# A Fourier transform ahead of a two-layer network: input folds written in place, and one more buffer for the units' differences

## The chip, the cores and the metric

The kernel runs on one core of one Trainium2 chip. The metric is the device time of one execution in microseconds (us); lower is better. A core has five engines that run beside each other: TensorE (PE in the profile, its weight loads PEld), VectorE (DVE), ScalarE (ACT), GpSimd (POOL) and SyncE (SP), which here only starts transfers (DMAs). SBUF is the working memory that all of them reach, PSUM the one in which TensorE puts its sums.

## The reference

```
x: (8, 3008, 256) f32, w_in: (256, 2048), w_out: (2048, 256)
X = fft(fft(x, axis=1), axis=2).real                 # (8, 3008, 256)
h = X.reshape(24064, 256) @ w_in                     # (24064, 2048)
g = where(h >= 1, h, where(h <= -1, 0, (h + 1)**2 / 4))
out = g @ w_out                                      # (24064, 256)
```

## The kernel before, in words

**The transform.** The host only reorders x. Per batch b, x comes in eight tiles `x_b_q` of 128 x 2 x 512 floats (512 KB each, `load_x`, line 126, DMA on line 130, issued by SyncE). A *fold* (`fold_x`, line 133) adds the two halves of a tile into `y_b_q` (line 138), 96 x 512; for q = 0 a second instruction takes their difference over 64 columns (`yd`, line 142). Folds run on GpSimd, but for four of the first batch, which run on VectorE. Stage 1 (`stage1_sums`, line 323) reads y with 4 matmuls for a tile (line 330), and the sums are copied to a tile z (line 360). Stage 2 (line 391) multiplies z (line 403) and splits the result into a high and a low part, `pqh` and `pql` (lines 177 and 178). `nyquist` makes one row a batch, written to DRAM and read back into `nyb` tiles (lines 383 and 388).

**The network.** Work is cut into *units* (b, k, f): batch, chunk k of 3 (482, 512 and 512 columns), and one of 16 groups of 128 hidden features; 384 units in all. `gemm1` (line 434) makes two PSUM tiles `uv` with three matmuls each (line 443), then VectorE makes `us` (line 446) and the two halves of `h`, us - uv and us + uv (lines 449 and 450): the unit's differences. ScalarE makes the tile `a` with two activations (lines 455 and 456). `activate` (line 459) has VectorE write min/max of a and h over h (line 470), ScalarE make `gh` of it (line 471) and GpSimd make `gl` = h - gh in two instructions (line 475); these last two are the last readers of h. `gemm2` (line 484) runs four units later and adds twelve matmuls (line 507) into four PSUM banks `acc`. When a chunk closes (its last f), the banks are evicted by VectorE and ScalarE (lines 514 to 518, traced at a raised priority, line 512) into `o` tiles, and stored (line 525).

**The weights** come as 64-bit floats in raw words and are converted in the first part of the run (`convert_*`, lines 205 to 247) on VectorE, ScalarE and GpSimd; w_in is multiplied with the second transform's matrix there (`fold_half`, line 286). `take_delta` (line 303) copies one row of that result to SBUF and `move_delta` (line 279) spreads it with four small DMAs over a column of `delta` (line 282). The first 24 units (`NATIVE`) multiply in full precision with one matmul in place of three.

**Buffers.** A tile is asked for with a tag, and a tag has a fixed number of buffers (`bufs`); whoever wants the next one waits until the last reader of the buffer's old content is done. Before the change: `y` has 3 buffers of 512 columns, shared by the folded tiles and the three rows of `take_delta`; `h` has 3 of 1024 columns, shared by the units and those converted weights that have no other place in `WORK` (line 103); `xt`, which the x tiles use, has 4, and four raw weight tiles pass through it too (line 102); x tiles 4 to 7 of the first batch lie in the four `gl` buffers.

**The order of the work.** The start is written out by hand: `START`, `AHEAD`, `AMID` and `STEPS` (lines 67 to 99) name steps by letter and number (`y1` and `g3` are folds, `p3` stage 1 of tile 3, `l12` a weight load, `r1` a delta row's DMAs), and `pin` (line 590) fixes the order of issue on each engine up to unit 24. From there on the framework's scheduler sets the order on each engine and on SyncE's queue, from priorities in the order of tracing and from when it takes operands and buffers to be free. The transform of the next batch is cut into pieces (`fft_pieces`, line 415) that are strewn between the units; `stage1` (line 365) folds a tile one piece ahead of its matmuls, and a load of tile q + 4 is traced right after the piece of tile q (lines 634 and 635). Batch 1's folds of tiles 0 to 3 are tied behind VectorE's latest instruction by hand (line 146).

Of the kernel before, what the change touches and what calls it, by code (L numbers as in the profile page):

```python
# [9 lines left out]
F32 = mybir.dt.float32  # L10
# [12 lines left out]
P = 128  # L23
XC = 8
GPC = 4
CH = 512
# [74 lines left out]
RAW = {0: "gh", 1: "gh", 2: "woh", 3: "woh", 4: "woh", 5: "woh", 6: "wol", 7: "wol", 8: "wol", 9: "wol"}  # L101
RAW |= {10: "xt", 11: "xt", 12: "xt", 13: "xt", 14: "pqh", 15: "pql"}
WORK = {1: "a", 3: "a", 4: "gl", 5: "gl", 7: "a", 8: "gl", 9: "gl", 11: "a", 12: "gl", 13: "gl", 15: "a"}
BUFS = {"h": 3, "a": 3, "gl": 4}

EARLY_BANKS = 12
BANK = {"s2_0_3": "acc3", "delta_1": "acc2"}
# [8 lines left out]
def fft_ffn_kernel(ctx: ExitStack, tc: tile.TileContext, x, cst, w_in, w_out, out):  # L116
# [3 lines left out]
    sb = ctx.enter_context(tc.tile_pool(name="sb", bufs=1))  # L120
# [12 lines left out]
    def fold_x(b, q, engine=None):  # L133

        t = xt.pop((b, q))
        engine = engine or nc.gpsimd
        y = sb.tile([96, CH], F32, tag="y", name=f"y_{b}_{q}", bufs=3)
        first = engine.tensor_tensor(y, t[:96, 0], t[:96, 1], op=ALU.add)  # L138
        yt[b, q] = y
        if q == 0:  # L140
            y = sb.tile([96, NA], F32, tag="yd", name=f"yd_{b}", bufs=1)
            engine.tensor_tensor(y, t[:96, 0, :NA], t[:96, 1, :NA], op=ALU.subtract)
            yt[b, "d"] = y
        return first.ins

    def fold_x_behind_vector(q):
        last = [ins for ins in traced if ins.engine == mybir.EngineType.DVE][-1]
        sync = mybir.DependencyInfo(mybir.DependencyClass.Sync, mybir.DependencyReason.DATA)
        tc.add_manual_dep(fold_x(1, q), last.name, sync, reason="beside VectorE's next steps")
# [55 lines left out]
    def convert_mantissa(n):  # L205
        raw = raws.pop(n)
        tag = WORK.get(n, "h")
        t = sb.tile([P, 2, CH], U32, tag=tag, name=f"cv_{n}", bufs=BUFS[tag])
        high = raw[:, :, 1]
# [91 lines left out]
        nc.scalar.activation(wh[m][:, cols], folds[n], AF.Copy, scale=inner if m else 1.0)  # L301

    def take_delta(f4):
        row = sb.tile([1, CH], F32, tag="y", name=f"row_{f4}", bufs=3)
        nc.scalar.activation(row, folds.pop(2 * f4 + 1)[0:1], AF.Copy)
        deltas[f4] = row

    def fold_low(n):
        f4, m = divmod(n, 2)
        cols = slice(f4 * CH, (f4 + 1) * CH)  # L310
        high = wh[m][:, cols].bitcast(F32)
        pt = folds.pop(n)
        if m == 1:
            nc.vector.scalar_tensor_tensor(wl[m][:, cols], pt, inner, high, op0=ALU.mult, op1=ALU.subtract)
            if f4:
                folds[n] = pt
                take_delta(f4)
        else:
            nc.vector.tensor_tensor(wl[m][:, cols], pt, high, op=ALU.subtract)
# [45 lines left out]
    def stage1(b, q):  # L365
        for p in range(q, min(q + 2, XC)):
            if (b, p) in xt and (b, p) not in yt:
                fold_x_behind_vector(p) if b == 1 and p < 4 else fold_x(b, p)
        stage1_sums(b, q)
        stage1_copy(b, q)  # L370
# [60 lines left out]
    def signs(i):  # L431
        return (slice(0, 1), slice(1, 2)) if i == n_units - 1 else (slice(0, 2),)

    def gemm1(i):
        b, k, f = units[i]
        n = WIDTH[k]
        hi, lo = pq[b, k]
        cols = slice(f * P, (f + 1) * P)
        uv = []
        for m in range(2):  # L440
            t = ps.tile([P, CH], F32, tag="uv", name=f"uv_{i}_{m}", bufs=3)
            for j, (w, r) in enumerate(((wh, hi), (wl, hi), (wh, lo))):
                nc.tensor.matmul(t[:, :n], w[m][:, cols], r[:, m, :n], start=(j == 0), stop=(j == 2))  # L443
            uv.append(t[:, :n])
        us = sb.tile([P, CH], F32, tag="us", name=f"us_{i}", bufs=2)[:, :n]
        nc.vector.scalar_tensor_tensor(us, nyb[b, k][:, :n], delta[:, f : f + 1], uv[0], op0=ALU.mult, op1=ALU.add)  # L446
        run_steps(AHEAD.get(i, ""))
        h = sb.tile([P, 2, CH], F32, tag="h", name=f"h_{i}", bufs=3)[:, :, :n]
        nc.vector.tensor_tensor(h[:, 0], us, uv[1], op=ALU.subtract)  # L449
        nc.vector.tensor_tensor(h[:, 1], us, uv[1], op=ALU.add)  # L450
        a = sb.tile([P, 2, CH], F32, tag="a", name=f"a_{i}", bufs=3)[:, :, :n]

        run_steps(AMID.get(i, ""))
        for sg in signs(i):
            nc.scalar.activation(a[:, sg], h[:, sg], AF.Relu, bias=half, scale=0.5)  # L455
            nc.scalar.activation(a[:, sg], a[:, sg], AF.Square)  # L456
        fronts[i] = h, a
# [82 lines left out]
    def piece_sums(n):  # L540
# [10 lines left out]
        "m": lambda n: nc.sync.dma_start(cm, cst[:, _OFF[2] :]),  # L551
        "x": lambda n: load_x(0, n),
        "y": lambda n: fold_x(0, n, nc.vector),
        "L": lambda n: load_x(1, n),
        "Y": fold_x_behind_vector,
# [27 lines left out]
    def run_steps(names):  # L583
        for s in names.split():
            steps[s[0]](int(s[1:] or 0))
# [17 lines left out]
    for i in range(n_units + LAG):  # L603
        if i < n_units:
            b, r = divmod(i, per)
            r0 = NEXT if b == 0 else 0
            if r == r0:
                pending = fft_pieces(b + 1) if b + 1 < NB else []
                done, total = 0, sum(w for w, _ in pending)
                if pending and b:  # L610
                    for q in range(4):
                        load_x(b + 1, q)
            gemm1(i)
            if b == 0 and units[i][2] == NFT - 2:
                load_parts(units[i][1])
            if 1 < i <= PINNED:
                activate(i - 1)
            if i >= PINNED:
                activate(i)
        first, _, then = STEPS.get(i, "").rpartition("|")  # L620
# [4 lines left out]
        if i < n_units:  # L625
            run_steps(then)
            change = units[i][2] == (FIRST if b == 0 else 0) + LAG
            while pending and (change or units[i][2] != (FIRST if b == 0 else 0) + LAG - 1 and done < total * (r + 1 - r0) / (per - r0)):
                change = False
                w, f = pending.pop(0)  # L630
# [65 lines left out]
```

## Time and profile before

| what | value |
|---|---|
| runs | 1738.72, 1739.39, 1734.0 us; median 1738.72 |
| the profiled execution | 1734.84 us, its span 1733.1 us |
| granted TensorE clock | 1.000 |
| TensorE | 1723.0 us busy, 99% of the span, 7804 matmuls |
| weight loads | 1392.1 us, 80% |
| VectorE | 1418.8 us, 82% |
| ScalarE | 1333.9 us, 77% |
| GpSimd | 1168.0 us, 67% |
| DMA | 80.89 MB, mean 47 GB/s |

The span reaches from the first to the last instruction; the time of the execution has a little more around it. Busy time is the time in which an engine had an instruction under way. A wait is idle time of an engine, put down to the instruction that ended it (`DVE h L449 <- POOL gl L475` is VectorE idle ahead of line 449 until a gl subtraction on GpSimd was done). Matmuls are pipelined and their ends are modelled, so two that follow each other overlap in the rows.

### The profile page before, as it was taken

The page shows a single profiled execution, that of the slowest core. Times are in us where ns is not written, and L with a number is a line of the kernel's source. Part 1 is how long each engine was busy: PE and PEld are TensorE (multiplying, and loading weights), DVE is VectorE, ACT ScalarE, POOL GpSimd, SP SyncE. Part 2 cuts the span into 40 slices and gives each one's busy share as a digit, 9 for nine tenths or more (in the row PEclk, how much of TensorE's full clock was granted, in tenths as well). Part 3 has the DMA queues.
Part 4 walks back from the last instruction along what each step waited for, and adds up shares of the span by engine and source line. Part 5 has one row for each costly group of instructions (what it writes and reads, how often), then busy time and mean ns, then how long its engine had stood idle before and what let it go on. Part 6 is the DMA issues. An engine that isn't in the chain of part 4 may idle for free.

```text
span 1733.1 us, 21482 instructions
## 1 busy us (share of the span) xinstructions
PE 1723.0 (99%) x7804; PEld 1392.1 (80%) x7804; DVE 1418.8 (82%) x1759; ACT 1333.9 (77%) x1561; POOL 1168.0 (67%) x801
## 2 busy tenths in 40 slices
PE   9999999999999999999999999999999999999998
PEld 6556888888888888888888888888888888888877
DVE  8997788888788887788887888878887788888886
ACT  6877777877778777887777777778778777777776
POOL 1125768776778667786678766778667766676775
PEclk9999999999999999999999999999999999999999
DMA  8133112110011100111011100111001000000000
GB/s 318 48 109 133 59 45 74 48 38 31 12 62 59 32 25 13 62 59 32 25 37 49 60 19 25 49 37 60 19 25 37 1 35 32 1 25 15 10 25 25
DMA packets 33738, 80.89 MB, mean 47 GB/s; under 512 B 4704, under 2 KB 9952, under 8 KB 33632
## 3 DMA queue, kind: packets, MB, share of 16 engines
q1 hardware_dynamic: 33596, 79.52, 13.2%
q8 instruction: 61, 1.00, 0.2%
q14 instruction: 45, 0.37, 0.1%
q10 hardware_dynamic: 36, 0.01, 0.0%
HBM read 51.70 MB, written 27.81 MB: 46 GB/s over the span
## 4 chain that ended last, share of the span: by engine, by line
PE 67%; ACT 20%; DVE 10%; issue 2%; DMA 0%; ACTq 0%; SPq 0%
PE acc L507 41%; PE uv L443 20%; DVE h L470 9%; ACT a L456 7%; ACT gh L471 7%; ACT a L455 5%; PE s L403 2%; PE s L330 2%; PE wps L293 1%; ACT z L360 1%; DVE h L450 0%; DVE h L449 0%; DMA raw<-in_moe_w_in_dram 0%; ACTq L471 0%; DVE o L518 0%
## 5 line engine op out<-in xcount | busy, mean ns | idle before, releaser
L475 POOL TENSOR_TENSOR gl<-h,gh 128x512 fp32r<-128x512 f32 (+1 forms) x716 | 1043.4, 1479 | 427.9 <-ACT gh L471 368.2
L470 DVE SCALAR_TENSOR_TENSOR h<-a,h 128x1024 f32<-128x1024 f32 (+2 forms) x361 | 541.5, 1500 | 237.1 <-ACT a L456 234.8
L471 ACT ACTIVATE gh<-h 128x1024 fp32r<-128x1024 f32 (+2 forms) x361 | 376.9, 1044 | 340.8 <-DVE h L470 317.4
L507 PE MATMUL acc<-gh,woh 128*128 128x512 f32 (+1 forms) x1440 | 570.2, 396 | 2.3 <-DVE o L518 2.2
L507 PE MATMUL acc<-gl,woh 128*128 128x512 f32 (+1 forms) x1440 | 563.6, 391 | 0.0
L507 PE MATMUL acc<-gh,wol 128*128 128x512 f32 (+1 forms) x1440 | 560.7, 389 | 0.0
L455 ACT ACTIVATE a<-h,biases 128x1024 f32<-128x1024 f32 (+1 forms) x385 | 431.8, 1122 | 23.3 <-DVE h L450 22.0
L456 ACT ACTIVATE a<-a 128x1024 f32<-128x1024 f32 (+1 forms) x385 | 399.4, 1037 | 7.6
L507 PEld LDWEIGHTS acc<-gh,woh 128*128 128x128 f32 x1440 | 270.7, 188 | 60.6 <-DVE o L518 5.7
L507 PEld LDWEIGHTS acc<-gl,woh 128*128 128x128 f32 x1440 | 271.3, 188 | 56.5
L507 PEld LDWEIGHTS acc<-gh,wol 128*128 128x128 f32 x1440 | 270.7, 188 | 54.7
L443 PE MATMUL uv<-pqh,wh 128*128 128x512 f32 (+1 forms) x768 | 308.6, 402 | 1.0 <-DVE h L450 1.0
L449 DVE TENSOR_TENSOR h<-us,uv 128x512 f32<-128x512 f32 (+1 forms) x384 | 260.0, 677 | 51.9 <-POOL gl L475 5.3
L443 PE MATMUL uv<-pql,wh 128*128 128x512 f32 (+1 forms) x768 | 299.2, 390 | 0.0
L443 PE MATMUL uv<-pqh,wl 128*128 128x512 f32 (+1 forms) x768 | 298.8, 389 | 0.0
L446 DVE SCALAR_TENSOR_TENSOR us<-nyb,delta,uv 128x512 f32<-128x512 f32 (+1 forms) x384 | 278.8, 726 | 10.8 <-PE uv L443 10.4
L450 DVE TENSOR_TENSOR h<-us,uv 128x512 f32<-128x512 f32 (+1 forms) x384 | 256.4, 668 | 0.0
L443 PEld LDWEIGHTS uv<-pqh,wh 128*128 128x128 f32 x768 | 144.2, 188 | 38.0 <-issue 4.3
L443 PEld LDWEIGHTS uv<-pqh,wl 128*128 128x128 f32 x768 | 144.2, 188 | 34.7 <-issue 5.4
L443 PEld LDWEIGHTS uv<-pql,wh 128*128 128x128 f32 x768 | 144.1, 188 | 30.2 <-DVE pql L178 0.4
L138 POOL TENSOR_TENSOR y<-x 96x512 f32<-96x512 f32 x60 | 108.1, 1802 | 25.9 <-PE s L330 14.0
L360 ACT ACTIVATE z<-s 64x192 f32<-64x192 f32 x240 | 81.7, 340 | 7.3 <-PE s L330 3.8
(64 smaller groups left out, 679.7 us busy)
## 6 DMA issues: line engine op xcount, KB each, us to landing
x<-in_x_dram SPq DMA_DIRECT2D x64, 512.0 KB, 3.5
out_dram<-o SPq DMA_DIRECT2D x26, 512.0 KB, 2.8
out_dram<-o SPq DMA_DIRECT2D x14, 482.0 KB, 2.9
nyb<-nyr SPq DMA_DIRECT2D x24, 256.0 KB, 3.3
raw<-in_moe_w_in_dram SPq DMA_DIRECT2D x4, 512.0 KB, 7.1
raw<-in_moe_w_out_dram SPq DMA_DIRECT2D x4, 512.0 KB
part<-o SPq DMA_DIRECT2D x4, 512.0 KB
os<-part SPq DMA_DIRECT2D x4, 512.0 KB, 5.8
```

What stands on the lines that cost most here:

```text
L138: first = engine.tensor_tensor(y, t[:96, 0], t[:96, 1], op=ALU.add)
L360: ins = nc.scalar.activation(dst, src, AF.Copy)
L443: nc.tensor.matmul(t[:, :n], w[m][:, cols], r[:, m, :n], start=(j == 0), stop=(j == 2))
L446: nc.vector.scalar_tensor_tensor(us, nyb[b, k][:, :n], delta[:, f : f + 1], uv[0], op0=ALU.mult, op1=ALU.add)
L449: nc.vector.tensor_tensor(h[:, 0], us, uv[1], op=ALU.subtract)
L450: nc.vector.tensor_tensor(h[:, 1], us, uv[1], op=ALU.add)
L455: nc.scalar.activation(a[:, sg], h[:, sg], AF.Relu, bias=half, scale=0.5)
L456: nc.scalar.activation(a[:, sg], a[:, sg], AF.Square)
L470: nc.vector.scalar_tensor_tensor(h[:, sg], a[:, sg], 1.0, h[:, sg], op0=ALU.min, op1=ALU.max)
L471: nc.scalar.activation(gh[:, sg], h[:, sg], AF.Copy)
L475: engine.tensor_tensor(gl[:, sg], h[:, sg], gh[:, sg].bitcast(F32), op=ALU.subtract)
L507: nc.tensor.matmul(acc[:, :n], w, g[:, sg], start=(begin and j == 0), stop=(last and j == len(terms) - 1))
```

## The change

For q = 1 to 7 the fold's sum is no longer put into a `y` tile but written over the tile's own first half, `t[:96, 0]`, and stage 1 reads it there. So the x buffer is held until those matmuls are done. For q = 0 a `y` tile stays, since the second instruction still needs both halves; `y` goes from 3 buffers to 1, still shared with the three rows of `take_delta`. The two buffers given up (512 floats a partition each) are as large as one `h` buffer, and `h` goes from 3 to 4, for the units and for the converted weights.

```
-BUFS = {"h": 3, "a": 3, "gl": 4}
+BUFS = {"h": 4, "a": 3, "gl": 4}
...
         t = xt.pop((b, q))
         engine = engine or nc.gpsimd
-        y = sb.tile([96, CH], F32, tag="y", name=f"y_{b}_{q}", bufs=3)
+        y = sb.tile([96, CH], F32, tag="y", name=f"y_{b}_{q}", bufs=1) if q == 0 else t[:96, 0]
         first = engine.tensor_tensor(y, t[:96, 0], t[:96, 1], op=ALU.add)
...
-        row = sb.tile([1, CH], F32, tag="y", name=f"row_{f4}", bufs=3)
+        row = sb.tile([1, CH], F32, tag="y", name=f"row_{f4}", bufs=1)
...
-        h = sb.tile([P, 2, CH], F32, tag="h", name=f"h_{i}", bufs=3)[:, :, :n]
+        h = sb.tile([P, 2, CH], F32, tag="h", name=f"h_{i}", bufs=4)[:, :, :n]
```

## The prediction

> **What bounds the kernel now.** I read the stretches first (columns: PE, weight loads, DVE, ACT, POOL, each with its busy us and its instructions, then the granted clock).
>
> ```profile
> core 0: us, PE busy (x) PEld busy (x) DVE busy (x) ACT busy (x) POOL busy (x), PEclk, DMA share, GB/s
> 0.00:25.00 25.00, 22.77 (x115) 15.29 (x116) 17.91 (x45) 14.39 (x33) 5.79 (x9) 1.00 0.89 329
> 25.00:150.00 125.00, 125.00 (x421) 74.06 (x421) 117.31 (x181) 98.41 (x135) 21.94 (x18) 1.00 0.30 107
> 150.00:1700.00 1550.00, 1546.64 (x7149) 1280.09 (x7149) 1261.93 (x1508) 1201.35 (x1373) 1125.85 (x766) 1.00 0.11 38
> 1700.00:1733.10 33.10, 28.55 (x123) 22.69 (x121) 21.68 (x27) 19.75 (x23) 14.39 (x10) 1.00 0.09 33
> ```
>
> Three regimes stand there. Up to 25 us the kernel loads. From 25 to 150 us VectorE is the tightest (117.31 of 125 us, while TensorE issues 421 matmuls, 3.4 in a us). From 150 us on TensorE is busy for 1546.64 of 1550 us and issues 4.6 in a us, at clock 1.00 throughout; VectorE has 288 us to spare there. A matmul that is held at its start can still count as busy, so I looked next at the waits between 165 and 1733 us: every wait of TensorE itself that sums to over 0.8 us (total us, times, longest), and those of the tiles that the change touches.
>
> ```profile
> POOL gl L475 <- PE acc L507: 48.5, 21, 2.3
> PEld acc L507 <- DVE o L518: 5.7, 10, 1.1
> DVE h L449 <- POOL gl L475: 5.3, 8, 1.1
> PEld uv L443 <- DVE h L450: 2.6, 6, 1.3
> POOL y L138 <- PE s L330: 2.4, 1, 2.4
> PE acc L507 <- DVE o L518: 2.2, 7, 0.6
> PEld ny L376 <- ACT a L455: 1.5, 4, 0.4
> PEld s L330 <- ACT z L360: 1.2, 4, 0.3
> PE uv L443 <- DVE h L450: 1.0, 2, 0.9
> PEld uv L443 <- DVE us L446: 1.0, 4, 0.3
> PEld acc L507 <- ACT o L516: 0.9, 2, 0.5
> ```
>
> The rows of TensorE (PE and PEld) sum to 16.1 us in 1568 us. Only 4.6 us of it (2.6 + 1.0 + 1.0) is a wait for the PSUM banks that the units' differences read. The row that the fourth buffer is aimed at is VectorE's own: it waited 5.3 us, in 8 places, for GpSimd to let go of an h tile. Last I read the chain that ended last, which is TensorE without a break up to the final eviction.
>
> ```profile
> 1714.60 13.96 PE acc L507 x60
> ```
>
> That busy TensorE is near its limit is borne out by its weight loads, which stand in the groups:
>
> ```profile
> L507 PEld LDWEIGHTS acc<-gl,woh 128*128 128x128 f32 x1440 | 271.3, 188 | 56.5
> L507 PEld LDWEIGHTS acc<-gh,woh 128*128 128x128 f32 x1440 | 270.7, 188 | 60.6 <-DVE o L518 5.7 <-ACT o L516 0.9 <-ACT a L455 0.6
> ```
>
> The idle time ahead of a load is 39 ns on average (56.5 us by 1440) in a group that names no releaser, and 42 ns in the one that names 7.2 us. It is a pitch that every load has, not a wait that a buffer ends, so I count the named waits alone. The Trainium skill's page "Perfetto Trace Analysis", section "Identifying the Most-Contended Engine", says that matmul busy time misleads and that the busy share of LDWEIGHTS tells the headroom. By that rule TensorE, with loads busy for 80% of the span, is not at its limit, and a wait taken from another engine could shorten the kernel in full; the trace speaks against it with the 39 ns.
>
> **The fourth buffer of h.** An h tile is written on lines 449 and 450, read by ScalarE, written over on 470, and freed by the second gl subtraction on GpSimd (475). With four, the write of unit i waits for gl of unit i-4 instead of i-3, so the 5.3 us of VectorE should go. That is not yet time: VectorE must have made TensorE late. The longest such case shows how it came about.
>
> ```profile
> 1159.67 0.66 DVE L449 TENSOR_TENSOR h<-us,uv 128x482 f32<-128x482 f32 x1
> 1161.53 2.58 DVE L470 SCALAR_TENSOR_TENSOR h<-a,h 128x964 f32<-128x964 f32 x1 [1.20 <-ACT a L456]
> 1164.03 0.65 DVE L450 TENSOR_TENSOR h<-us,uv 128x482 f32<-128x482 f32 x1
> ```
>
> The older unit's L470 stands between the two halves of the newer unit's h, waits 1.20 us for ScalarE, runs long, and L450 frees its bank only after 1164.03, 3.7 us after L449 ended. There the order on VectorE, which the scheduler chooses outside the written-out start, made the wait, not a missing h buffer. A fourth buffer lets the scheduler place L449 and L450 earlier, and may undo some of these cases. The gain is therefore between 0 and 4.6 us; I take 1.5 us, about a third, since the one case that I can follow (1.3 of the 4.6) had its h tile in hand.
>
> The other side of the same step: if L449 and L450 go first, L470 comes later by up to one pair, and with it gh and gl.
>
> ```profile
> L450 DVE TENSOR_TENSOR h<-us,uv x384: 643/675/685, 26.8 to 1717.4; 128x512 f32<-128x512 f32 x128, 128x482 f32<-128x482 f32 x64
> L470 DVE SCALAR_TENSOR_TENSOR h<-a,h x361: 687/1476/2683, 146.3 to 1722.8; 128x1024 f32<-128x1024 f32 x124, 128x964 f32<-128x964 f32 x56, 128x512 f32<-128x512 f32 x1
> ```
>
> A pair is about 1.35 us (2 x 0.675, min/median/max in ns). What covers it is that gl is made early: the first wait row has GpSimd waiting 48.5 us, 21 times, for TensorE to give back a gl buffer, and no row has TensorE waiting for gh or gl. Cost 0; if that cover were gone, each such unit would cost TensorE up to 1.35 us.
>
> **The fold in place.** Lines 137 and 138 keep the same instruction, shape and count on the same engine; only the destination changes, for q = 1 to 7.
>
> ```profile
> L138 POOL TENSOR_TENSOR y<-x 96x512 f32<-96x512 f32 x60 | 108.1, 1802 | 25.9 <-PE s L330 14.0 <-DVE wol L262 6.7 <-DVE cv L216 2.5
> 12.81 5.09 POOL L138 TENSOR_TENSOR y<-x 96x512 f32<-96x512 f32 x4 [11.55 <-PE s L330]
> x<-in_x_dram SPq DMA_DIRECT2D x64, 512.0 KB, 3.5
> ```
>
> No row shows an in-place fold. L470 above writes over one of its inputs on another engine, at 1476 ns for twice the columns; it gives no reason for a price either way. Bounds: between a fold of the four at the start (1.27 us, 5.09 by 4) and the mean of all (1.80 us) lies 0.53 us, so 60 folds could move by 32 us of GpSimd up or down, an engine that has 424 us to spare between 150 and 1700 us (1550 less 1125.85). On the end: 0.
>
> What does move is who frees what. Now a fold waits for a y buffer, which the matmuls of three tiles earlier free. After the change it waits only for its load, and that load waits for the matmuls of four tiles earlier rather than for their fold. On a middle batch (SyncE, TensorE, GpSimd, TensorE):
>
> ```profile
> 346.20 13.80 SPq L130 DMA_DIRECT2D x<-in_x_dram  x2
> 482.18 1.03 PE L330 MATMUL s<-cs,y 96*128 96x96 f32 x8
> 495.23 2.23 POOL L138 TENSOR_TENSOR y<-x 96x512 f32<-96x512 f32 x1
> 532.97 1.03 PE L330 MATMUL s<-cs,y 96*128 96x96 f32 x8
> ```
>
> The sixth tile's load goes out at 346.2 us today. Changed, it waits for the second tile's matmuls, which end at 483.2 us, and lands 3.5 us later, at 486.7. Its fold runs at 495.2 today and TensorE reads it at 533.0. So a load 137 us later is still 8.5 us ahead of the fold and, less 2.2 us for a fold, 44 us ahead of its reader: cost 0, and 44 us is the cover. Behind the waiting load on SyncE's queue stand output stores, nyr and nyb. They are queued by the same scheduler that sees the new release time, so I expect the load to be queued later rather than to hold them; if it does hold them, a store has until the next chunk closes, about 67 us: 16 units of 4.18 us, the 6 matmuls of uv and 12 of acc that follow each other in the chain.
>
> ```profile
> 1709.03 1.39 PE uv L443 x6
> 1710.42 2.79 PE acc L507 x12
> ```
>
> **The single y buffer.** It holds each batch's first fold and the three rows of the delta column. Two rows are gone long before the next; the tight place is the last row, whose four small DMAs must land before batch 1's first fold may write.
>
> ```profile
> 116.19 2.41 SPq L282 DMA_DIRECT2D delta<-row  x4
> 120.91 1.27 POOL L138 TENSOR_TENSOR y<-x 96x512 f32<-96x512 f32 x1 [2.51 <-DVE cv L216]
> 133.34 1.03 PE L330 MATMUL s<-cs,y 96*128 96x96 f32 x8
> DMA to landing us min/median/max: 1.9/2.0/2.0
> ```
>
> The last of them is issued by 118.6 and lands by about 120.6; the fold starts at 120.91, held by VectorE anyway, and is read at 133.34. Cost 0, between a gain of nothing and 1 us that stays hidden.
>
> **The start.** The first folds on GpSimd run back to back (the row from 12.81 on), and the slots of the x tiles go on to weight loads:
>
> ```profile
> 16.59 3.77 PE L330 MATMUL s<-cs,y 96*128 96x96 f32 x32
> 24.74 1.59 SPq L200 DMA_DIRECT2D raw<-in_moe_w_in_dram  x2
> ```
>
> The matmuls that will free the slots end at 20.4 us; the weight loads that take them leave at 24.7. The order there is written out and stays. VectorE, which bounds 25 to 150 us, loses and gains no instruction, and has no h wait in that stretch. Cost 0, and no gain.
>
> **Sum.** Against its own time the profiled run (1734.84 us, span 1733.1) becomes 1734.84 - 1.5 + 0 + 0 + 0 = 1733.3 us. That run lies 3.9 us below the median of the runs shown (1738.72, of 1734.0 to 1739.39), so for the median I say 1737.2 us.
>
> **The rivals.** *Faster.* The schedule is made anew, and a freer VectorE also reaches the evictions at the chunk closings sooner. The waits on these (5.7 + 2.2 + 0.9) and on h (4.6) hold 13.4 us; half of it gone is 6.7 us, 1732.0 us. For it: all of these end on VectorE or ScalarE, where order is everything. Against: from 150 us on VectorE is busy for 81% of the time, and the evictions already have a raised priority (line 512).
>
> *Slower.* The same new order puts an L449 and L450 pair of the next unit ahead of an eviction. TensorE needs those banks at once at a closing, so a pair there costs 1.35 us in full.
>
> ```profile
> L518 DVE COPY o<-acc 128x512 f32<-128x512 f32 (+1 forms) x48 | 32.0, 672 | 2.4 <-PE acc L507 2.4
> ```
>
> 48 copies, two at a closing, make 24 closings, 3 of them in the start. It decides from 4 of the 21 on (5.4 us); at 8 it adds 10.8 us, 1749.5 us. For it: at these closings TensorE already waits in 17 places. Against: the priority, and the mean of such a wait, 0.46 us (7.9 by 17), less than a pair. The Trainium skill's "SBUF — State Buffer", section "Who interferes with whom", adds a way to it: a VectorE instruction with two SBUF inputs contends with GpSimd's reads. By that rule L470 (a and h) may meet more of gl and the folds. The trace agrees so far as L470 goes up to 2683 ns and L450, with one input in PSUM, never over 685.
>
> *VectorE's wait counts in full.* Its 5.3 us come straight off the end, as they would if TensorE were not the bound: 1733.4 us, just beyond what a measurement tells. For it: weight loads leave TensorE's load path idle for some 40 ns each; against: the chain's end, and that only 4.6 us of TensorE's waits lie on what h frees. It is the rule of the Trainium skill's "Perfetto Trace Analysis" above that would have it so.
>
> *Nothing happens.* The h tiles wait on gl in 8 units only, and if the scheduler issues VectorE in the order of today, the fourth buffer stands empty: 1738.7 us.
>
> **How the numbers follow.** Forecast 0.54, nothing 0.10, faster 0.18, VectorE's wait in full 0.04, slower 0.14. A measurement of this kernel tells some 0.3%, or 5.2 us, from no change; the forecast and the last rival lie within it, so 0.22 faster, 0.64 same, 0.14 slower. The range goes from 1730 us (the faster rival's 1732.0 and a little of its other half) to 1743 us (three closings at 1.35 us above the highest run, 1739.39).
>
> **What would show it.** Right: the row of h waiting for gl is gone, TensorE's busy time from 150 to 1700 us stays within 2 us, its waits sum to 12 to 17 us, folds of a batch's last tiles come after loads that leave behind the matmuls of four tiles earlier, and the single y buffer makes no wait over 1 us. Wrong: a row in which TensorE waits for gl or for y, closings with waits over 1 us, output stores standing behind x loads so long that an eviction waits for its o tile, or a stretch from 25 to 150 us that is longer or shorter by over 2 us.

## The result, and the profile after

The change makes the kernel slower: the median goes from 1734.7 us (6 runs, 1732.1 to 1739.39) to 1757.92 us (6 runs, 1755.02 to 1765.07), a ratio of 1.0139 with a 95% interval of 1.0123 to 1.0155. The forecast was 1737.2 us in a range of 1730 to 1743; the time lies outside it. The profiled execution took 1756.21 us, its span is 1754.4 us at a granted clock of 1.000, so the comparison below is with the span of 1733.1 us. Three of the six runs after (1759.61 to 1765.07 us) had a mean granted clock of 0.997, the other three (1755.02 to 1756.23 us) one of 1.000.

The stretches of after come first, cut at the same times (columns as before: PE, weight loads, DVE, ACT, POOL).

```profile
0.00:25.00 25.00, 23.11 (x115) 15.41 (x116) 17.99 (x45) 14.32 (x33) 5.79 (x9) 1.00 0.91 327
25.00:150.00 125.00, 125.00 (x421) 74.11 (x421) 118.63 (x181) 98.23 (x135) 23.82 (x20) 1.00 0.30 107
150.00:1700.00 1550.00, 1533.13 (x7058) 1259.36 (x7057) 1264.19 (x1488) 1184.82 (x1358) 1084.86 (x753) 1.00 0.11 38
1700.00:1754.40 54.40, 49.92 (x215) 39.97 (x214) 39.03 (x47) 34.86 (x38) 30.74 (x21) 1.00 0.05 20
```

The first two rows issue what they issued before (115 and 421 matmuls): the loss is all in the third, where TensorE issues 7058 matmuls in place of 7149, at the same clock. GpSimd, whose instructions the change touches, has no more to do: over the span the page gives it 1145.2 us of busy time, 22.8 less than before. So time was lost in waits. The largest of TensorE between 165 and 1755 us, with two of GpSimd (total us, times, longest):

```profile
POOL gl L475 <- PE acc L507: 34.7, 15, 2.3
PEld uv L443 <- DVE h L450: 21.4, 29, 1.5
POOL x L138 <- DMA x<-in_x_dram: 15.4, 8, 5.2
PE uv L443 <- DVE h L450: 11.1, 17, 1.1
PEld acc L507 <- DVE o L518: 7.5, 15, 1.1
PEld uv L443 <- DVE us L446: 2.8, 8, 0.4
PE acc L507 <- DVE o L518: 2.3, 8, 0.6
PEld s L403 <- DVE pql L178: 2.3, 1, 2.3
```

VectorE's wait for an h tile (5.3 us before) has no row any more: the fourth buffer does what it says. In its place TensorE waits for L450 to let go of the uv banks, 21.4 us on its weight loads and 11.1 us on its matmuls (the two rows describe partly the same places), where it was 2.6 and 1.0 us. New is also that a fold on GpSimd waits for its load, 15.4 us in 8 places. The closings (`o`) hardly moved.

Where the time was lost can be laid against the units. I took the start of each unit's first uv matmul in both traces (a batch has 48 units; batches are numbered from 0, so the third is batch 2, and between its units lies batch 3's stage 1). After falls behind by 21.4 us in all. 4.3 us of it come in units 34 to 42, where TensorE waits in batch 1's stage 2 (the last of the rows above, 2.3 us for VectorE, and 1.7 us more for ScalarE). 17.0 us come in units 0 to 24 of the batches from the second on, where the next batch's stage 1 and its folds are strewn between the units; nearly nothing is lost elsewhere. In the third batch the steps of over 0.2 us are units 12 and 13 (0.26 and 1.26 us), 18 (0.75), 19 (0.68) and 21 (0.67).

On VectorE one group grew, L470. Its row in after, with the folds in place and L470's neighbours, and then its row in before:

```profile
L470 DVE SCALAR_TENSOR_TENSOR h<-a,h 128x1024 f32<-128x1024 f32 (+2 forms) x361 | 561.3, 1555 | 236.4 <-ACT a L456 233.4
L138 POOL TENSOR_TENSOR x<-x 96x512 f32<-96x512 f32 x53 | 81.5, 1538 | 37.6 <-DMA x<-in_x_dram 31.6
...
L449 DVE TENSOR_TENSOR h<-us,uv 128x512 f32<-128x512 f32 (+1 forms) x384 | 259.7, 676 | 48.2 <-DVE us L446 1.5
L450 DVE TENSOR_TENSOR h<-us,uv 128x512 f32<-128x512 f32 (+1 forms) x384 | 255.9, 667 | 0.0
```

```profile
L470 DVE SCALAR_TENSOR_TENSOR h<-a,h 128x1024 f32<-128x1024 f32 (+2 forms) x361 | 541.5, 1500 | 237.1 <-ACT a L456 234.8
```

L470 takes 19.8 us more over the same 361 instructions, while L449 and L450 keep their means. (The folds in place take 1.54 us on average, against 1.80 us for the folds before, so folding in place is no dearer by itself.) The 361 did not all get a little slower: 11 took over 1.9 us before, 28 do after. One of these, in the timeline of after (start, length, engine, line; in brackets the idle time ahead and what ended it), GpSimd first, then VectorE, then TensorE:

```profile
517.62 3.35 POOL L475 TENSOR_TENSOR gl<-h,gh 128x482 fp32r<-128x482 f32 x2 [2.55 <-ACT gh L471]
520.93 1.29 POOL L138 TENSOR_TENSOR x<-x 96x512 f32<-96x512 f32 x1
522.19 2.42 POOL L475 TENSOR_TENSOR gl<-h,gh 128x482 fp32r<-128x482 f32 x2
...
523.22 2.40 DVE L470 SCALAR_TENSOR_TENSOR h<-a,h 128x964 f32<-128x964 f32 x1 [0.80 <-ACT a L456]
525.55 0.65 DVE L450 TENSOR_TENSOR h<-us,uv 128x482 f32<-128x482 f32 x1
...
524.89 0.38 PE L507 MATMUL acc<-gl,woh 128*128 128x482 f32 x1
526.25 0.49 PE L443 MATMUL uv<-pqh,wh 128*128 128x482 f32 x1 [0.97 <-DVE h L450]
```

The same unit before:

```profile
508.00 2.22 POOL L138 TENSOR_TENSOR y<-x 96x512 f32<-96x512 f32 x1
510.60 5.89 POOL L475 TENSOR_TENSOR gl<-h,gh 128x482 fp32r<-128x482 f32 x4 [0.38 <-ACT gh L471]
...
516.20 1.32 DVE L470 SCALAR_TENSOR_TENSOR h<-a,h 128x964 f32<-128x964 f32 x1 [0.80 <-ACT a L456]
517.43 0.65 DVE L450 TENSOR_TENSOR h<-us,uv 128x482 f32<-128x482 f32 x1
```

Read it from the top. In after a fold stands at 520.93 right ahead of a gl pair, so the pair runs from 522.19 to 524.61 and not a fold's length earlier. L470 of a younger unit, ready at 523.22 as it was ready at 516.20 before (0.80 us behind ScalarE both times), now begins while the pair runs, and ends 1.0 us after it. L450 stands behind L470 on VectorE and frees its bank 1.1 us late. TensorE starts uv 1.36 us after its last acc matmul in place of 0.22. Before, the pairs were over at 516.49 and L470 met only a tail of 0.3 us.

What L470 costs when GpSimd is idle is in before's groups by form: L464 is the same operation on the same columns, in the first 24 units, which have no gl.

```profile
L470 DVE SCALAR_TENSOR_TENSOR h<-a,h 128x964 f32<-128x964 f32 x112 | 161.3, 1440 | 87.1 <-ACT a L456 86.9
...
L464 DVE SCALAR_TENSOR_TENSOR g<-a,h 128x964 f32<-128x964 f32 x16 | 18.5, 1158 | 0.0
```

A unit of 482 columns takes 3.93 us on TensorE (uv at 514.97 and at 518.90 before). Where L470 and the gl pair do not overlap, they need 1.16 + 2.42 = 3.58 us of that, which leaves 0.35 us in a unit. That L470 waits for GpSimd shows in nearly every row: of the 112 L470 on 964 columns in after, 102 end between 1.00 and 1.04 us after a GpSimd instruction ends (16 of the 17 that take over 1.9 us), and four take about the 1.16 us that they take alone. The Trainium skill's page "SBUF — State Buffer", section "Who interferes with whom", has a VectorE instruction with two SBUF inputs contend with GpSimd's reads, and the one that issues first decides who blocks. The trace agrees on both counts: L470 is stretched and L449 and L450, which read one of their inputs from PSUM, are not; and where L470 was there first the fold was the one that ran long (2.22 us at 508.00, against 1.29).

Why do the folds stand elsewhere? The order of instructions on TensorE, VectorE and ScalarE is the same in both kernels; only GpSimd's and SyncE's differ. Counted in units whose gl pair stands ahead of them on GpSimd (the first 24 units, which have none, are counted in), the eight folds of this stretch stood at 95, 99, 101, 104, 108, 111, 115 and 118 before, and stand at 100, 102, 105, 109, 110, 112, 116 and 119 now (96 is the third batch's first). The late units follow four or five pairs behind four of these: 105 is unit 9 of the batch and unit 13 is late (the case above), 109, 110 and 112 are units 13, 14 and 16, and 18, 19 and 21 are late. Tile 3 of batch 3 shows the cause: before, its fold ran at 468.06, after the matmuls of tile 0 (over at 465.55) gave back its y buffer; now it runs at 356.90, right behind a gl pair and without a wait. Three y buffers had been pacing the folds.

### The profile page after: what moved, and what is told of

Same layout as the page of the kernel before. It is cut to its first block, busy times and chain, and to the rows that moved or that the text cites. A ratio compares the mean times of both kernels' runs of the same rounds, so it can differ in the third digit from the quotient of the medians.

```text
span 1754.4 us, 21535 instructions
## 1 busy us (share of the span) xinstructions
PE 1731.2 (99%) x7804; PEld 1388.9 (79%) x7804; DVE 1439.8 (82%) x1759; ACT 1332.2 (76%) x1561; POOL 1145.2 (65%) x801
## 4 chain that ended last, share of the span: by engine, by line
PE 67%; ACT 18%; DVE 11%; issue 3%; DMA 0%; ACTq 0%; SPq 0%; DVEq 0%
PE acc L507 41%; PE uv L443 20%; DVE h L470 9%; ACT a L456 7%; ACT gh L471 6%; ACT a L455 5%; PE s L403 2%; PE s L330 2%; DVE h L450 1%; ACT z L360 1%; PE wps L293 1%; DVE h L449 1%; DMA x<-in_x_dram 0%; DVE os L514 0%; DVE o L518 0%
## 5 line engine op out<-in xcount | busy, mean ns | idle before, releaser
L470 DVE SCALAR_TENSOR_TENSOR h<-a,h 128x1024 f32<-128x1024 f32 (+2 forms) x361 | 561.3, 1555 | 236.4 <-ACT a L456 233.4
L443 PE MATMUL uv<-pqh,wh 128*128 128x512 f32 (+1 forms) x768 | 311.5, 406 | 11.4 <-DVE h L450 11.1
L449 DVE TENSOR_TENSOR h<-us,uv 128x512 f32<-128x512 f32 (+1 forms) x384 | 259.7, 676 | 48.2 <-DVE us L446 1.5
L443 PE MATMUL uv<-pql,wh 128*128 128x512 f32 (+1 forms) x768 | 299.1, 389 | 0.0
L443 PE MATMUL uv<-pqh,wl 128*128 128x512 f32 (+1 forms) x768 | 298.9, 389 | 0.0
L446 DVE SCALAR_TENSOR_TENSOR us<-nyb,delta,uv 128x512 f32<-128x512 f32 (+1 forms) x384 | 278.3, 725 | 15.0 <-PE uv L443 14.3
L450 DVE TENSOR_TENSOR h<-us,uv 128x512 f32<-128x512 f32 (+1 forms) x384 | 255.9, 667 | 0.0
L443 PEld LDWEIGHTS uv<-pqh,wh 128*128 128x128 f32 x768 | 144.1, 188 | 60.0 <-DVE h L450 21.8
L443 PEld LDWEIGHTS uv<-pqh,wl 128*128 128x128 f32 x768 | 144.2, 188 | 32.7 <-issue 5.4
L443 PEld LDWEIGHTS uv<-pql,wh 128*128 128x128 f32 x768 | 144.1, 188 | 30.4 <-DVE pql L178 0.4
L138 POOL TENSOR_TENSOR x<-x 96x512 f32<-96x512 f32 x53 | 81.5, 1538 | 37.6 <-DMA x<-in_x_dram 31.6
```

The lines of the kernel that those rows point to most:

```text
L470: nc.vector.scalar_tensor_tensor(h[:, sg], a[:, sg], 1.0, h[:, sg], op0=ALU.min, op1=ALU.max)
```

## The experiments

Two theories stood at the start: A, that the folds' new places on GpSimd make the loss, and B, that the fourth h buffer does, through the order made with it. Later ones are named where they come. Medians are in us and ratios to the kernel before on the same chip, with 95% intervals.

**The change with three h buffers.**

```
-BUFS = {"h": 4, "a": 3, "gl": 4}
+BUFS = {"h": 3, "a": 3, "gl": 4}
```

> Folds in place as in the change, but three h buffers again. If the places of the folds on GpSimd make the loss (theory A: a fold ahead of a unit's two gl subtractions moves them onto VectorE's L470, and L450 frees the uv banks late), nothing comes back: 1750 to 1765 us, TensorE's waits for L450 still some 30 us, against 3.6 us in the kernel before, and VectorE's wait for an h tile is back with some us. If the fourth h buffer makes it (theory B), the time returns to 1731 to 1740 us.

1759.87, ratio 1.0151 (1.0135 to 1.0167). The loss is whole without the fourth buffer, so B falls. Waits of this kernel:

```profile
PEld uv L443 <- DVE h L450: 24.5, 33, 1.7
PE uv L443 <- DVE h L450: 12.2, 17, 1.3
...
DVE h L449 <- POOL gl L475: 7.0, 9, 1.9
```

**The whole change, and the wait of the y ring put back by hand.** From batch 1 on a fold waits for the last stage-1 matmul of the fold three before it, as three y buffers made it. (Six or seven lines are added: L470 is L477 there, L443 is L450, L450 is L457.)

```
+        folded.append((b, q))
+        if b and len(folded) > 3:
+            sync = mybir.DependencyInfo(mybir.DependencyClass.Sync, mybir.DependencyReason.DATA)
+            tc.add_manual_dep(first.ins, summed[folded[-4]].name, sync, reason="as with three y buffers")
...
+        summed[b, q] = last.ins
```

> The whole change, with one wait put back: from batch 1 on a fold also waits for the matmuls that read the fold three before it, as three y buffers made it wait. Theory A: folds stand where they stood before, so 1730 to 1740 us, L470 at a mean of about 1500 ns instead of 1555, TensorE's waits for L450 under 6 us. Theory B (fourth h buffer) and theory C (folding in place, or the later loads, costs by itself): 1750 to 1765 us, as in the changed kernel.

1738.51, ratio 1.0022 (1.0008 to 1.0036): about 20 of the 23 us are gone. Waits, and the group of L470:

```profile
PEld uv L450 <- DVE h L457: 4.2, 10, 1.3
...
PE uv L450 <- DVE h L457: 1.7, 2, 0.9
```

```profile
L477 DVE SCALAR_TENSOR_TENSOR h<-a,h 128x1024 f32<-128x1024 f32 (+2 forms) x361 | 543.8, 1506 | 236.2 <-ACT a L463 233.5
```

L470 is back from 561.3 to 543.8 us, and 11 of them take over 1.9 us, as before. The missing wait is the cause; A holds. B falls again, and so does theory C, that folding in place or the later loads cost by themselves: both are still in this kernel. What remained open was by which way: the time that folds take, their wait for a load, or both.

**The first tile in place too.** The difference is taken first, then the sum is written over the first half, so this tile holds its x buffer like the others and no load follows at once on its fold.

```
-        y = sb.tile([96, CH], F32, tag="y", name=f"y_{b}_{q}", bufs=1) if q == 0 else t[:96, 0]
+        y = t[:96, 0]
```

> The whole change, and the first tile of a batch folded in place too (its difference first), so that its x buffer is not handed on at once to the load of the tile after next batch's first, whose fold then waits on GpSimd for the landing. Theory A1 (GpSimd standing still for a landing, 31.6 us in the changed kernel, is the larger part): 1738 to 1748 us with that wait under 12 us. Theory A2 (the places themselves are the larger part, landing or not): 1750 to 1760 us.

1750.85, ratio 1.0095 (1.0079 to 1.011): at the edge of the second of the forecasts. It takes the folds at 109 and 110 apart (they stand at 105, 109 and 112 now) and lowers GpSimd's waits for loads from 15.4 us to about 8.4, but it changes both at once and so doesn't separate them.

**Folds in the same places, but short.** For batches 2 to 7 and all tiles but the first, only 64 of the 512 columns are summed; the rest of the sum is left out here.

```
+        w = CH if b < 2 or q == 0 else NA
+        first = engine.tensor_tensor(y[:, :w], t[:96, 0, :w], t[:96, 1, :w], op=ALU.add)
```

> The whole change, with the folds of batches 2 to 7 and tiles 1 to 7 cut to 64 of 512 columns (the rest of the sum is left out); GpSimd, like every engine, has the same order of instructions as in the changed kernel, and the loads stay. Theory A2 (a fold of 1.3 us ahead of a unit's gl moves it onto L470): most of the 23 us goes, 1734 to 1745 us, with what batch 1 lost (4 us) left. Theory A1 (GpSimd stands still for the landing of a load): 1750 us and over.

1735.18, ratio 1.0012 (1.0001 to 1.0023), with GpSimd's instructions in the order of the change. (Lines are one higher.) The waits and L470's group:

```profile
POOL x L139 <- DMA x<-in_x_dram: 15.4, 9, 4.9
```

```profile
L471 DVE SCALAR_TENSOR_TENSOR h<-a,h 128x1024 f32<-128x1024 f32 (+2 forms) x361 | 537.1, 1488 | 228.4 <-ACT a L457 225.4
```

GpSimd waits 15.4 us for loads as in the whole change, and it costs nothing. TensorE's wait for L450 has no row. So it is the 1.3 us that a fold takes on GpSimd in that place. **The same cut with the ring's wait:**

> The control for the short folds: the same cut in the kernel with the third wait put back (folds at the old places, 1738.5 us when whole). Under theory A2 short folds make little of a difference there, 1733 to 1740 us, and it is within 5 us of the short folds at the new places; under theory A1 the short folds at the new places are 10 us or more above it.

1731.63, ratio 0.9992 (0.998 to 1.0005). With nearly nothing to fold, either order ends within 0.2% of the kernel before. So the places matter only through the time that the folds take there; at the old places whole folds take 0.3% more than these short ones (1.0022 against 0.9992).

**Folds tied behind VectorE's latest instruction,** for batches 2 to 7, the way the kernel does it by hand for four tiles of batch 1, to see whether another pacing does as well.

```
-                fold_x_behind_vector(p) if b == 1 and p < 4 else fold_x(b, p)
+                fold_x_behind_vector(p, b) if b > 1 or p < 4 else fold_x(b, p)
```

> The whole change, with every fold from batch 2 on tied behind VectorE's latest instruction at the place where it is traced, as batch 1's first four are: folds come later, next to their matmuls, right behind an L470, in the time in which GpSimd waits for ScalarE's gh anyway. Theory A: fewer L470 over 1.9 us than 28, near the 11 of before, and 1728 to 1742 us. Theory B or C: 1750 us and over, since the buffers and the fold in place are the same.

1780.96, ratio 1.0271 (1.0254 to 1.0289), the worst of all, and the expectation missed. Folds now come too late, and TensorE waits for them:

```profile
PEld s L330 <- POOL y L138: 27.1, 6, 5.2
PE s L330 <- POOL y L138: 24.5, 6, 4.8
PEld s L330 <- POOL x L138: 7.0, 6, 2.8
```

In this kernel the order on TensorE and ScalarE differs too, where stage 1 stands at other places. That says nothing against the pacing by y, only that the tie must not come later than the reader allows.

**The price of 1.25 us on GpSimd by itself.** In the kernel before, without the change, the first gl subtraction is made a second time in 4 units of batches 1 to 6, 24 in all, and r is the number of the unit in its batch of 48. First in the stretch of stage 1, then later, where no stage 1 runs:

```
+        twice = 1 <= units[i][0] <= 6 and i % per in (9, 11, 13, 15)
+        for sg in (0, 0, 1) if twice else (0, 1):
```

> The kernel before, with one price put in by itself: in batches 1 to 6 the first gl subtraction of the units 9, 11, 13 and 15 of the batch (inside the stretch in which stage 1's pieces run) is done twice, 24 GpSimd instructions of some 1.25 us more; nothing else moves. Theory A: each pushes a gl pair onto an L470, L450 is late, TensorE waits; 0.5 to 1.2 us each, 1746 to 1764 us. Theory C (places of GpSimd's work do not matter, the change's cost lies in the loads or in the fold in place): 1731 to 1740 us, since GpSimd has over 400 us to spare.

1750.04, ratio 1.0093 (1.0077 to 1.0109): 16 us for 24 instructions, 0.7 us each, with nothing of the change in the kernel. 19 of L470 take over 1.9 us. But part of it goes another way than in the change: VectorE waits 18.6 us for h tiles that GpSimd gives back late, and most of TensorE's waits are then behind L446 (14.2 and 9.5 us), not behind L450 (5.5 and 2.0).

> The same 24 instructions in the units 33, 35, 37 and 39 of the batch, where no stage 1 piece runs and the chunk is 512 columns wide. Theory A, if it takes stage 1's extra work on ScalarE and VectorE to make the collision count: under 8 us, 1731 to 1742 us. If a collision costs the same wherever it falls: as in the run before, 1746 to 1764 us.

With r = 33, 35, 37, 39: 1745.94, ratio 1.0071 (1.0052 to 1.0091), 12.4 us, where under 8 was expected. The theory that only the stretch of stage 1 makes such an instruction dear fell here. The next theory, D, was that it is the closeness: folds or doubled subtractions in a row are dear anywhere, apart they are free.

> As the two runs with 24 doubled gl subtractions, but in the units 28, 33, 38 and 43 of the batch, five apart. Theory D (a unit's gl pair and its L470 run one after the other, 2.6 + 1.2 of a unit's 4.18 us, so that GpSimd has some 0.3 us a unit in which to catch up, and a further 1.25 us costs only when it is not caught up before the next such work): most is caught up, under 8 us, 1731 to 1741 us. If every such instruction costs the same wherever it stands: 12 to 16 us as in the runs before, 1745 to 1752 us.

With r = 28, 33, 38, 43: 1734.04, ratio 1.0001 (0.9991 to 1.001). Five units apart, the same 24 instructions are free.

> The same 24 in the units 33, 34, 35 and 36 of the batch, one after the other. Theory D: nothing is caught up between them; with 4 x 1.25 us less the same 0.3 us a unit, more than with every second unit (12 us): 1750 to 1770 us. If every one costs the same: 1744 to 1752 us.

With r = 33 to 36, each behind the other: 1741.67, ratio 1.0043 (1.0028 to 1.0058). Dear, but below both forecasts and less than every second unit, where D wanted more: D fell in that form. Both had VectorE waiting for an h tile. First the row of every second unit, then that of the four in a row:

```profile
DVE h L449 <- POOL gl L476: 23.2, 26, 1.2
```

```profile
DVE h L449 <- POOL gl L476: 15.7, 20, 1.2
```

**Folds bunched by hand.** The whole change, with the next batch's tiles 0 to 3 held until the last stage-1 matmul of the batch under way, so that five folds stand nearly in a row at the end of the stretch.

```
+        if b > 1 and q < 4:
+            sync = mybir.DependencyInfo(mybir.DependencyClass.Sync, mybir.DependencyReason.DATA)
+            tc.add_manual_dep(first.ins, summed[b - 1, XC - 1].name, sync, reason="after the batch ahead")
```

> The whole change, with the folds of tiles 0 to 3 of the next batch held until the last stage 1 matmul of the batch under way, so that none of them falls into the stretch of stage 1; they then stand in a row of four or five at one place. If the stretch of stage 1 is what makes a fold dear: 1733 to 1742 us. Theory D (folds in a row are dear anywhere): 1745 to 1765 us.

1765.55, ratio 1.0181 (1.0164 to 1.0198), as D had it. The timeline of this kernel (GpSimd, then VectorE; L470 is L476):

```profile
578.36 1.29 POOL L140 TENSOR_TENSOR y<-x 96x512 f32<-96x512 f32 x1
579.62 2.54 POOL L140 TENSOR_TENSOR x<-x 96x512 f32<-96x512 f32 x2
582.12 3.53 POOL L481 TENSOR_TENSOR gl<-h,gh 128x512 fp32r<-128x512 f32 x2
585.61 2.54 POOL L140 TENSOR_TENSOR x<-x 96x512 f32<-96x512 f32 x2
588.11 6.00 POOL L481 TENSOR_TENSOR gl<-h,gh 128x512 fp32r<-128x512 f32 x4
...
586.58 2.65 DVE L476 SCALAR_TENSOR_TENSOR h<-a,h 128x1024 f32<-128x1024 f32 x1 [0.67 <-ACT a L462]
591.39 3.80 DVE L476 SCALAR_TENSOR_TENSOR h<-a,h 128x1024 f32<-128x1024 f32 x1 [0.68 <-ACT a L462]
```

The second L470 begins beside four gl instructions that follow each other without a break until 594.11. It takes 3.80 us and ends 1.1 us after them.

**The fourth h buffer at the old places.** The kernel with the ring's wait, with three h buffers again:

> Folds in place at the old places, with three h buffers: the last corner of the square of fold places and h buffers. Theory A and D: the h buffers are worth nothing that can be measured, so within 4 us of the same kernel with four (1738.5): 1734 to 1743 us. If the fourth h buffer helps at the old places: 1743 us and over.

1734.35, ratio 1.0004 (0.9995 to 1.0013). This closes a square: old places with three h 1.0004 and with four 1.0022; new places with three 1.0151 and with four 1.0139. The places are worth 1.2 to 1.5%; the buffer nothing that these runs can tell, though the wait that it removes is back here (5.6 us, 8 times).

**The doubled subtractions with four h buffers,** in the kernel with the ring's wait, to see by which way they cost. Every second unit outside the stretch of stage 1:

> The 24 doubled gl subtractions in every second unit (33, 35, 37, 39), now in the kernel with folds in place at the old places and four h buffers (1738.5 us by itself). In the kernel before, with three, they cost 12.4 us, and VectorE waited 23.2 us for h tiles. If the cost goes through the h tiles that GpSimd gives back late: under 5 us over 1738.5, up to 1743 us, and no such wait. If it goes through L470 running while gl runs (theory A): the same 10 to 14 us, 1748 to 1753 us.

1736.41, ratio 1.0015 (1.0005 to 1.0026): free beside the 1.0022 of the kernel that it is built on. Four in a row:

> The same 24 in four units in a row (33 to 36), with four h buffers. With three they cost 7.5 us. Through the h tiles: under 3 us, up to 1742 us. Through L470: 6 to 9 us, 1744 to 1748 us. The catching up of theory D alone would have it dearer than every second unit.

1736.15, ratio 1.0009 (0.9993 to 1.0025): free as well. So outside the stretch of stage 1 the cost with three buffers (12.4 and 7.5 us) went through late h tiles, and the fourth buffer takes it away. (The kernels compared also differ in the fold in place, whose folds stand at the places of before.) In the stretch of stage 1:

> The 24 in the units 9, 11, 13 and 15, in the stretch of stage 1, with four h buffers; with three they cost 16 us, of which TensorE's waits behind VectorE's L446 and L450 made most. Through the h tiles: under 6 us, up to 1745 us. Through L470: 13 to 19 us, 1751 to 1758 us.

1749.88, ratio 1.0088 (1.0067 to 1.0109), 11.4 us above the kernel that it is built on, and between the two forecasts. Its waits, and L470's group:

```profile
PEld uv L450 <- DVE h L457: 14.6, 19, 1.7
PE uv L450 <- DVE h L457: 8.3, 11, 1.3
```

```profile
L477 DVE SCALAR_TENSOR_TENSOR h<-a,h 128x1024 f32<-128x1024 f32 (+2 forms) x361 | 554.3, 1535 | 236.7 <-ACT a L463 234.1
```

That is the picture of the change itself: no h tile is late, L470 is long (554.3 us in place of 543.8), and L450 gives back the banks late. There the fourth buffer takes away VectorE's wait for h (18.6 us with three) and at most some 5 us of the cost (an estimate: 16 less 11.4); the larger part stays.

## Why the prediction was wrong

**The step that failed** is "The fold in place": "On the end: 0", and of the moved load "cost 0, and 44 us is the cover". The cover was right and answered another question. Nothing waits for a fold: in the whole change no row has TensorE waiting for x or y after 165 us. The step asked when a fold is ready and when it is read, and never where it would then stand on GpSimd's queue, and ahead of what. It saw that "a fold waits for a y buffer" and that this wait goes, and took the wait for a cost that falls away; it had been a spacing that was worth about 20 us (1738.51 against 1757.92; by the ratios, 1.0022 against 1.0139).

**GpSimd's "424 us to spare"** was the wrong measure. With 24 instructions added in every second unit the kernel lost 16 us in the stretch of stage 1 and 12.4 us after that stretch; with the same 24 five units apart, after that stretch too, none. What is to spare is about 0.35 us in a unit of 482 columns, beside L470. By that a fold of 1.29 us needs nearly four such units to be absorbed (an estimate, 1.29 / 0.35). The old places are 2 to 4 pairs apart, the new ones 1 to 4.

**The longest wait was misread.** The prediction followed the case at 1161.53 on VectorE alone and found that "the order on VectorE ... made the wait". GpSimd's rows of before at that time show what made the larger part of it:

```profile
1159.40 1.29 POOL L138 TENSOR_TENSOR y<-x 96x512 f32<-96x512 f32 x1
1160.66 2.42 POOL L475 TENSOR_TENSOR gl<-h,gh 128x482 fp32r<-128x482 f32 x2
```

A fold, a gl pair right behind it, and L470 of 2.58 us beside them: the mechanism of the loss stood in the row that was quoted. The words "runs long" passed over it; 2.58 us against a median of 1.476 asked for a look at the other engine.

**The fourth buffer.** The wait of 5.3 us on h did go, as said. The gain of 1.5 us didn't come, and VectorE's order did not change at all, so neither the gain through a new order nor the two rivals that lived on one (evictions reached sooner, evictions reached later) could happen. Of the buffer taken by itself the rival *Nothing happens* was right about the time. *VectorE's wait counts in full* is refuted by the square above: with the ring's wait, the h wait is there (three buffers) or not (four), and the kernel is not slower with it. The number 1737.2 also stood on a median of three runs, 1738.72; that of six is 1734.7.

**The slower rival** had the right sign and the wrong place. Its price of 1.35 us an event was of the right size (1.14 us in the case above, 1.0 us on average if the 17.0 us are put on the 17 more of L470 that take over 1.9 us, and 0.7 us for a doubled subtraction in the stretch of stage 1, some of it through h tiles), but the closings stayed where they were (7.5 + 2.3 us after, 5.7 + 2.2 before). Its sentence that L470 may meet more of gl and the folds names the cause, and was given neither a count nor a price.

**What was right.** The stretch from 25 to 150 us kept its 421 matmuls, the single y buffer made no wait, and loads of a batch's later tiles leave behind the matmuls of four tiles earlier (tile 5 of batch 3 at 491.05, after matmuls that end at 488.82). The two signs that were named for being right and failed, TensorE's busy time within 2 us (it fell by 13.5) and waits of 12 to 17 us (those behind L450 alone are 32.5), pointed at L450 at once.

**What is shown and what isn't.** Shown: the missing y wait makes 20 of the 23 us; it does so by the time that folds take where they then stand; extra time on GpSimd in that stretch costs 16 us with nothing of the change, and 11.4 us with four h buffers, where no h tile is late. That L470 is slowed by sharing with GpSimd is read from its durations and ends beside GpSimd's rows; taking one of its SBUF inputs away wasn't tried. Open stays why some folds pay and others don't (the one at 105 pays, three pairs behind the one at 102, and those at 104, 108 and 111 before, as close, paid nothing), so the 0.35 us is no rule by which to place them; why four doubled subtractions in a row cost less with three h buffers (7.5 us) than every second unit (12.4 us), and whether the 0.2% of the change with the ring's wait is real: it arises from unit 36 to 72, and the interval of the version with three buffers (up to 1.0013) overlaps its own (from 1.0008). No complete version was found that beats the kernel before.

## What to carry to other kernels

Before a buffer wait is taken away, ask what the freed instruction will stand ahead of on its in-order queue: a small ring of tiles can be what spaces one engine's work. Spare time of an engine over the whole span is not spare time beside another engine: add up, for one period of the loop, what the two can't do together, and compare it with the period. And an instruction in a quoted row that takes far more than its median is the thing to explain, with the other engines' rows of the same microseconds.

## What the runs showed of the hardware

The length of L470 (128 x 964, two SBUF inputs) goes with what GpSimd still has to run without a break when it begins: 1.16 us with GpSimd idle, 1.32 us with 0.3 us of a pair left (516.20 of before), 2.40 us with 1.4 us left (523.22 of after) and 2.88 us with 1.9 us left (545.25 of after). In the last three it ends 1.0 us after GpSimd does. In the case above a fold of 1.29 us ahead of the pair so lengthened L470 by 1.08 us (2.40 against 1.32). The longest on 964 columns takes 3.35 us in after, and 4.53 us in the kernel with the ring's wait, where it begins beside a fold and a gl pair that follow each other.

The tie behind VectorE showed a second price of a wait. Its stretches around one fold that came late (columns as above):

```profile
690.00:698.00 8.00, 8.00 (x37) 6.61 (x36) 6.43 (x9) 6.31 (x7) 5.94 (x4) 1.00 0.01 2
698.00:704.00 6.00, 2.00 (x9) 1.57 (x9) 1.95 (x3) 2.62 (x3) 5.41 (x5) 0.86 0.10 20
704.00:709.00 5.00, 5.00 (x15) 4.00 (x15) 0.84 (x2) 2.77 (x7) 1.95 (x2) 0.50 0.21 83
```

TensorE is idle for 4 of the 6 us from 698, and then runs at a granted clock of 0.50: 15 matmuls in 5 us. After another such wait, of 4.82 us, uv matmuls of 482 columns start 0.40 us apart (924.76, 925.16, 925.56) in place of 0.22, until 927.6. The mean granted clock of this run is 0.988, by which at most some 21 of its 1780 us are the clock's (an estimate, 0.012 of 1780). The Trainium skill's page "TensorE: Matmul & The Clock Gate", section "Part 1: The HAM clock gate (the "warmup" mystery)", has the clock halved after an idle window of about 3.4 us; the trace agrees, with 0.50 after 4.82 us. But in these runs shorter waits were enough. In the kernel with the folds bunched by hand TensorE waits 2.11 us, until 379.88, and then runs at half the clock:

```profile
376.00:380.60 4.60, 2.49 (x11) 1.65 (x10) 4.48 (x3) 1.28 (x2) 2.29 (x3) 0.99 0.42 115
380.60:384.00 3.40, 3.40 (x14) 3.11 (x13) 2.74 (x4) 2.92 (x3) 2.38 (x2) 0.51 0.02 5
```

Another wait of 2.13 us there, from 593.71, left the clock at 1.00; what decides between the two is not shown. In the profiled execution of the change the clock stays at 1.00, and TensorE's longest wait after the first 30 us is 1.84 us.
